# Attention and two MLP blocks on one core: a weight's split issued earlier, an addition moved to ScalarE, the sinks' split in two

## The chip, the cores and the metric

The kernel runs on one NeuronCore of a Trainium2 chip. Five engines work side by side, each through its own queue in order: TensorE (PE, matrix products and transposes into PSUM), VectorE (DVE), ScalarE (ACT), GpSimd (POOL) and SyncE (SP, which issues most of the DMAs). The metric is the device time of one execution in microseconds; lower is better.

## The reference

Attention with sink tokens and a sliding window (2 batches, 8 heads, 768 positions, head size 64), then two MLP blocks on the result:

```
scores = scale * q @ k^T, kept where pos < n_sink or 0 <= rel < window, else -1e9
a = exp(scores - max);  a = a / (sum(a) + 1e-9);  x = a @ v          # n_sink 4, window 128
h = relu(x @ w_in);  u, v = halves of h;  v = layernorm(v)           # 512 -> 1024
x = (u * (w_spatial @ v + b_spatial)) @ w_out
u = x + (relu(x^T @ w_tok1) @ w_tok2)^T;  out = u + relu(u @ w_ch1) @ w_ch2
```

The MLP weights arrive as 64-bit floats. The kernel decodes them to fp32 on the chip and then splits each into a high part (rounded to the PE's fp32r) and a low part (the rest), so that one product is three passes: high by high, high by low, low by high.

## The kernel before

**The attention loop.** `banded` (L339 on) walks over 12 blocks of 128 positions, two phases of four heads each, so over 24 steps g, in a software pipeline with one iteration n per step, n = -3 to 25. Iteration n does, in the order in which it is issued (and each engine takes its own part of that order):

- `sums(n+1)`: on DVE the row sums plus 1e-9 (L195) and their reciprocal (L196).
- `a_transpose(n)`, `a_out(n)`: PE transposes the probabilities `e` into the PSUM tile `tr`; ACT copies it to `aT` (L275), DVE writes a masked copy `aL` (L278; not in a batch's first block, so not in iterations 0, 1, 12 and 13).
- `norm(n+1)`: `e` times the reciprocal, two heads on POOL (L246), two on ACT (L250).
- `qk(n+3)`, `scores(n+3)`: PE products into the PSUM tiles `sc`; DVE masks, scales and takes the row minima (L213, L218).
- `expo(n+2)`: four exponentials on ACT with their row sums (L234; the sums are read out by an instruction of their own, ACTIVATION_READ_ACCUMULATOR).
- in even iterations `v_step` (POOL, `dv`, the difference of two blocks' values, L285) and `sink_parts` (ACT L257, POOL L258 and L259, tile `eS`).
- in iterations 1 and 13 `split_vs`: the sinks' values `vs`, of which ACT makes the high part (L156) and DVE the low part (L158), from the raw tile that a DMA brought. They are first read by `sinks_mm` in iterations 4 and 16.
- `step`: one further part of each layer norm under way (DVE L547; later ACT L550, POOL L551).
- in iterations -1 to 6 (`PUMPS`) `pump`: one 128x512 piece of `w_in` is decoded on DVE in three steps (L481, L485, L488) into `wi`; then `flush` splits the piece decoded one iteration **before**: high part by an ACT copy (L499), low part by a POOL subtraction (L500). The piece just decoded waits in `self.half`; the last one is flushed in iteration 7.
- `pv(n-1)`: products with the values into `pv`; in even iterations then `sinks_mm`, and `x_out`: ACT copies `pv` to the high part `xTH` (L329), DVE subtracts for the low part `xTL` (L330). The `pv` bank is single, so the next block's first product waits for `xTL`.
- in odd iterations `sinks`: PE transposes `eS` (tile `fl`), ACT copies it to `aS` (L313).
- `fill`: groups of three PE products of the first MLP layer (`psv`, `psu`), as many as a budget allows, once their rows of x are there. Their PSUM tiles share two banks with `fl`.

Iterations -1 to 6 therefore carry the decoding on DVE, iterations 3 on the fill products on PE. The order is that of the code; no scheduler changes it. A weight's raw tile is double (`bufs=2`), so the load of piece w+2 is issued on SP when piece w is decoded.

**The rest.** After the loop `mlp` runs the remaining layers. The change doesn't touch it.

Of the kernel before, what the change touches and what calls it, by code (L numbers as in the profile page):

```python
# [8 lines left out]
F32R = mybir.dt.float32r  # L9
I32 = mybir.dt.int32  # L10
U32 = mybir.dt.uint32
AF = mybir.ActivationFunctionType
ALU = mybir.AluOpType
PSUM = bass.MemoryType.PSUM

P = 128
B, H, S, D = 2, 8, 768, 64
NB = S // P
DM = H * D
# [5 lines left out]
SK = 8  # L25
SR = 3 * 4 * SK
# [3 lines left out]
NG = B * NB * 2  # L30

LQ, LE, LN = 3, 2, 1
PUMPS = range(-1, 7)
# [3 lines left out]
def f32(ap):  # L37
    return ap.bitcast(F32)


class Kernel:
# [106 lines left out]
            nc.sync.dma_start(out=raw[0:SR], in_=self.vs[b])  # L148
            self.vsraw = raw

    def split_vs(self, b):

        nc = self.nc
        raw = self.vsraw
        t = self.vsb[b] = self.ap.tile([P, DM], F32R, name="vs", tag="vs", bufs=1)
        nc.scalar.activation(out=t[0:SR], in_=raw[0:SR], func=AF.Copy)  # L156
        r = slice(4 * SK, 8 * SK)
        nc.vector.tensor_tensor(out=t[r], in0=raw[r], in1=f32(t[r]), op=ALU.subtract)  # L158

    def slots(self, j):  # L160

# [28 lines left out]
    def sums(self, g):  # L190

        V = self.nc.vector
        r = self.ap.tile([P, 4], F32, name="r", tag="r", bufs=3)
        self.rs[g] = r
        V.tensor_scalar(out=r, in0=self.sm[g], scalar1=1e-9, scalar2=None, op0=ALU.add)  # L195
        V.reciprocal(r, r)  # L196

    def scores(self, g):

# [23 lines left out]
    def expo(self, g):  # L223
        nc = self.nc
        j, ph = divmod(g, 2)
        i = j % NB
        u = KW if i else P
        s, nm = self.ss[g]
        if ph == 0:
            self.e[j] = self.ap.tile([P, H, KW], F32, name="e", tag="e", bufs=2)  # L230
        sm = self.ap.tile([P, 4], F32, name="sums", tag="sums", bufs=3)
        self.sm[g] = sm
        for c in range(4):
            nc.scalar.activation(  # L234
                out=self.e[j][:, 4 * ph + c, :u], in_=s[:, c, :u], func=AF.Exp, bias=nm[:, c : c + 1], scale=-1.0,
                accum_out=sm[:, c : c + 1],
            )

    def norm(self, g):

        nc = self.nc
        j, ph = divmod(g, 2)
        r = self.rs[g]
        w = KW if j % NB else P
        e = self.e[j][:, 4 * ph : 4 * ph + 4, 0:w]
        nc.gpsimd.tensor_tensor(  # L246
            out=e[:, 2:4], in0=e[:, 2:4], in1=r[:, 2:4].unsqueeze(2).to_broadcast([P, 2, w]), op=ALU.mult
        )
        for c in range(2):
            nc.scalar.activation(out=e[:, c], in_=e[:, c], func=AF.Copy, scale=r[:, c : c + 1])  # L250

    def sink_parts(self, j):

# [85 lines left out]
    def banded(self):  # L339
        self.q, self.vb, self.vsb, self.ps_s, self.ss, self.e, self.sm, self.rs = {}, {}, {}, {}, {}, {}, {}, {}  # L340
        self.aT, self.ps_x, self.aS, self.dv, self.eS = {}, {}, {}, {}, {}
        NJ = B * NB
        self.kr = self.ap.tile([P, NC4, RING, KW], F32, name="kr")
        self.vf = self.ap, "vf", 2
        self.scalar_loads(self.cp)
        self.load_qk(0, 2)
        self.warm(10)
        self.load_qk(1)
        self.prefetch()
        self.load_v(0)  # L350
        self.load_qk(2)
        self.masks(self.ap)
        for n in range(-LQ, NG + 2):
            j, ph = divmod(n, 2)
            self.xdone = self.xnext
            if ph and n >= -1:
                if (n + 7) // 2 < NJ:
                    self.load_qk((n + 7) // 2)
                if (n + 3) // 2 < NJ:
                    self.load_v((n + 3) // 2)  # L360
            if 0 <= n + LN < NG:
                self.sums(n + LN)
            if 0 <= n < NG:
                self.a_transpose(n)
                self.a_out(n)
            if 0 <= n + LN < NG:
                self.norm(n + LN)
            if n + LQ < NG:
                self.qk(n + LQ)
                if n < 0:  # L370
                    self.warm(3)
                self.scores(n + LQ)
            if 0 <= n + LE < NG:
                self.expo(n + LE)
            if 0 <= n < NG and ph == 0 and j % NB:
                self.v_step(j)
                self.sink_parts(j)
            if n in (1, 13):
                self.split_vs(n // 12)
            self.step()  # L380
            if n in PUMPS:
                self.pump()
            if n == max(PUMPS) + 1:
                self.flush()
            if 0 <= n - 1 < NG:
                self.pv(n - 1)
                if ph == 0:
                    if (j - 1) % NB:
                        self.sinks_mm(j - 1)

                    self.fill_until(j - 1)
                    self.x_out(j - 1)
            if 0 <= n < NG and ph == 1 and j % NB:
                self.sinks(j)
            if n == NG - 4:
                self.raws = [self.spatial_load(r) for r in range(2)]
            self.fill(BUDGET)
        self.xdone = self.xnext
        self.vf = self.sp, "tmp", 4
# [529 lines left out]
```

## Time and profile before

| | us |
|---|---|
| median of 3 runs | 494.08 (492.68 to 495.11) |
| the profiled execution | 494.1 |
| its span, first to last instruction | 492.3 |
| PE busy in the span | 469.2 (95%) |
| DVE, ACT, POOL busy | 281.2, 178.8, 146.7 |

The profile is of one execution; times of rows are us from the start of its span. The share of busy time over the whole span hides the stages: the attention loop takes about the first 145 us, the MLP the rest. In the table by stretches, PEclk is the granted TensorE clock as a share of 2.4 GHz, so 0.50 is 1.2 GHz.

### The profile page before, as it was taken

How to read it: one execution, taken by the hardware profiler on the slowest of the kernel's cores; microseconds unless marked ns; L12 is line 12 of the kernel's file. 1: busy time of each engine (PE TensorE's matmuls, PEld its weight loads, DVE VectorE, ACT ScalarE, POOL GpSimd, SP SyncE). 2: the span in 40 equal slices, each digit the busy share in tenths (PEclk: the TensorE clock that was granted, in tenths of full speed). 3: DMA queues.
4: the chain of work that ended last, by engine and by line, in shares of the span. 5: the costliest groups of instructions: out<-in, count | busy, mean ns of one | idle time of the engine just before them, and what ended most of it. 6: DMA issues, size and time to landing. Idle time of an engine off the chain costs nothing.

```text
span 492.3 us, 6952 instructions
## 1 busy us (share of the span) xinstructions
PE 469.2 (95%) x2562; PEld 392.3 (80%) x2562; DVE 281.2 (57%) x633; ACT 178.8 (36%) x483; POOL 146.7 (30%) x164
## 2 busy tenths in 40 slices
PE   8678899999999999999999989999999999999994
PEld 7356588788898999998888768888888888888883
DVE  5899865775555399937878698666412211311112
ACT  4656777787754323225642122222101210010000
POOL 1355752354354556642543033222100000000000
PEclk9859899999999999999999999999999999999998
DMA  8744132202005023303534044222010000200002
GB/s 258 246 151 152 66 101 95 87 22 87 1 30 185 1 85 87 102 6 116 173 119 137 35 129 128 91 94 73 21 66 1 0 1 0 86 1 0 1 0 92
DMA packets 19722, 38.48 MB, mean 78 GB/s; under 512 B 1824, under 2 KB 8224, under 8 KB 19680
## 3 DMA queue, kind: packets, MB, share of 16 engines
q1 hardware_dynamic: 19248, 37.69, 23.5%
q8 instruction: 22, 0.36, 0.3%
q10 hardware_dynamic: 432, 0.26, 0.2%
q14 instruction: 20, 0.16, 0.1%
HBM read 34.80 MB, written 3.15 MB: 77 GB/s over the span
## 4 chain that ended last, share of the span: by engine, by line
PE 81%; DVE 11%; ACT 5%; issue 1%; POOL 1%; POOLq 0%; ACTq 0%
PE pso L60 7%; PE pso L58 7%; PE pso L59 7%; PE psc L58 6%; PE psc L60 6%; PE psc L59 6%; PE psg L60 3%; PE psg L59 3%; PE psg L58 3%; PE pv L301 3%; PE ps L60 2%; PE ps L58 2%; PE ps L59 2%; ACT e L234 2%; DVE wi L485 2%; PE psu L58 2%
## 5 line engine op out<-in xcount | busy, mean ns | idle before, releaser
L647 DVE SCALAR_TENSOR_TENSOR hh<-psc,hh 128x512 fp32r<-128x512 f32 x36 | 24.9, 691 | 124.6 <-ACT hh L646 124.6
L646 ACT ACTIVATE hh<-psc 128x512 fp32r<-128x512 f32 x36 | 21.5, 597 | 156.0 <-PE psc L60 156.0
L60 PE MATMUL pso<-c2H,hh 128*128 128x512 f32 x144 | 56.3, 391 | 1.9 <-DVE hh L647 1.9
L58 PE MATMUL pso<-c2H,hh 128*128 128x512 f32 x144 | 56.8, 394 | 0.0
L59 PE MATMUL pso<-c2L,hh 128*128 128x512 f32 x144 | 56.1, 390 | 0.0
L488 DVE SCALAR_TENSOR_TENSOR wi<-rawi,wi 128x512 int32<-128x512 int32 (+2 forms) x46 | 40.3, 876 | 1.6
L234 ACT ACTIVATE e<-s,nm 128x136 f32<-128x136 f32 (+1 forms) x96 | 37.6, 393 | 3.9 <-DVE nm L218 3.9
L485 DVE SCALAR_TENSOR_TENSOR wi<-rawi,wi 128x512 int32<-128x512 int32 (+2 forms) x46 | 36.4, 791 | 1.6
L481 DVE TENSOR_SCALAR wi<-rawi 128x512 int32<-128x512 int32 (+2 forms) x46 | 33.4, 726 | 0.7 <-DMA rawi<-in_moe_w_ch 0.5
L60 PEld LDWEIGHTS pso<-c2H,hh 128*128 128x128 f32 x144 | 27.0, 188 | 8.0 <-DVE hh L647 2.3
L58 PE MATMUL psg<-wsTH,vnH 128*128 128x384 f32 x96 | 32.1, 334 | 0.0
L59 PE MATMUL psg<-wsTL,vnH 128*128 128x384 f32 x96 | 32.1, 334 | 0.0
L60 PE MATMUL psg<-wsTH,vnL 128*128 128x384 f32 x96 | 32.1, 334 | 0.0
L500 POOL TENSOR_TENSOR c2L<-wi,c2H 128x512 fp32r<-128x512 f32 x12 | 16.1, 1339 | 52.4 <-ACT c2H L499 52.4
L59 PEld LDWEIGHTS pso<-c2L,hh 128*128 128x128 f32 x144 | 27.1, 188 | 5.4
L58 PEld LDWEIGHTS pso<-c2H,hh 128*128 128x128 f32 x144 | 27.0, 188 | 5.3
L188 PE MATMUL sc<-kr,q 64*128 64x264 f32 (+2 forms) x192 | 28.8, 419 | 0.4 <-DVE nm L218 0.2
L60 PE MATMUL psc<-u2H,c 128*128 128x512 f32 x72 | 28.0, 389 | 0.0
L58 PE MATMUL psc<-u2H,c1H 128*128 128x512 f32 x72 | 28.0, 389 | 0.0
L59 PE MATMUL psc<-u2L,c1H 128*128 128x512 f32 x72 | 28.0, 389 | 0.0
L60 PE MATMUL psc<-u2H,c1L 128*128 128x512 f32 x72 | 28.0, 389 | 0.0
L58 PE MATMUL psc<-u2H,c 128*128 128x512 f32 x72 | 28.0, 389 | 0.0
(143 smaller groups left out, 1120.1 us busy)
## 6 DMA issues: line engine op xcount, KB each, us to landing
rawi<-in_moe_w_ch SPq DMA_DIRECT2D x24, 512.0 KB, 3.4
rawi<-in_moe_w_in SPq DMA_DIRECT2D x8, 512.0 KB, 4.5
v<-in_v SPq DMA_DIRECT2D x12, 256.0 KB, 3.6
out_x<-o SPq DMA_DIRECT2D x12, 256.0 KB, 2.4
kr<-in_k SPq DMA_DIRECT2D x11, 272.0 KB, 4.1
q<-in_q SPq DMA_DIRECT2D x11, 256.0 KB, 4.2
raws<-in_w_spT SPq DMA_DIRECT2D x6, 384.0 KB, 4.5
rawi<-in_moe_w_out SPq DMA_DIRECT2D x4, 512.0 KB, 5.2
```

What stands on the lines that cost most here:

```text
L58: self.nc.tensor.matmul(ps, lh, rh, start=(first and i == 0), stop=False)
L59: self.nc.tensor.matmul(ps, lh, rl, start=False, stop=False)
L60: self.nc.tensor.matmul(ps, ll, rh, start=False, stop=(last and i == n - 1))
L188: nc.tensor.matmul(o, q[r, p, :], k, start=True, stop=True)
L234: nc.scalar.activation(out=self.e[j][:, 4 * ph + c, :u], in_=s[:, c, :u], func=AF.Exp, bias=nm[:, c : c + 1], scale=-1.0, accum_out=sm[:, ...
L301: nc.tensor.matmul(ps[h * D : (h + 1) * D, p, :], w[:, (2 * p + h) * D : (2 * p + h + 1) * D], self.aT[g][c][:, 2 * x + h, :], start=(p == ...
L481: V.tensor_scalar(out=wi, in0=hi, scalar1=3, scalar2=0x3FFFFFFF, op0=ALU.logical_shift_left, op1=ALU.bitwise_and,)
L485: V.scalar_tensor_tensor(out=wi, in0=hi, scalar=-0x40000000, in1=wi, op0=ALU.bitwise_and, op1=ALU.bitwise_or)
L488: V.scalar_tensor_tensor(out=wi, in0=lo, scalar=29, in1=wi, op0=ALU.logical_shift_right, op1=ALU.bitwise_or)
L500: self.nc.gpsimd.tensor_tensor(out=dl, in0=w, in1=f32(dh), op=ALU.subtract)
L646: nc.scalar.activation(out=h, in_=ps, func=AF.Relu)
L647: nc.vector.scalar_tensor_tensor(out=l, in0=ps, scalar=0.0, in1=f32(h), op0=ALU.max, op1=ALU.subtract)
```

## The change

Three edits, all in the attention loop.

1. `flush` leaves `pump`'s place in the iteration. A piece decoded in iteration n is now split in iteration n+1 behind `a_out` and POOL's part of `norm`, and ahead of ACT's part of `norm`. For that `norm` gets an argument and is called twice.
2. 1e-9 is added to the row sums on ACT, right behind the exponentials that made them, instead of on DVE ahead of the reciprocal.
3. `split_vs` is done in two iterations: ACT's part in 2 and 14, DVE's in 3 and 15.

```diff
-    def split_vs(self, b):
+    def split_vs(self, b, part):
...
-        t = self.vsb[b] = self.ap.tile([P, DM], F32R, name="vs", tag="vs", bufs=1)
-        nc.scalar.activation(out=t[0:SR], in_=raw[0:SR], func=AF.Copy)
-        r = slice(4 * SK, 8 * SK)
-        nc.vector.tensor_tensor(out=t[r], in0=raw[r], in1=f32(t[r]), op=ALU.subtract)
+        if part == 0:
+            t = self.vsb[b] = self.ap.tile([P, DM], F32R, name="vs", tag="vs", bufs=1)
+            nc.scalar.activation(out=t[0:SR], in_=raw[0:SR], func=AF.Copy)
+        else:
+            t = self.vsb[b]
+            r = slice(4 * SK, 8 * SK)
+            nc.vector.tensor_tensor(out=t[r], in0=raw[r], in1=f32(t[r]), op=ALU.subtract)
...
-        V.tensor_scalar(out=r, in0=self.sm[g], scalar1=1e-9, scalar2=None, op0=ALU.add)
-        V.reciprocal(r, r)
+        V.reciprocal(r, self.sm[g])
...
+        nc.scalar.activation(out=sm, in_=sm, func=AF.Copy, bias=1e-9)
...
             if 0 <= n + LN < NG:
-                self.norm(n + LN)
+                self.norm(n + LN, "P")
+            if n - 1 in PUMPS:
+                self.flush()
+            if 0 <= n + LN < NG:
+                self.norm(n + LN, "A")
...
-            if n in (1, 13):
-                self.split_vs(n // 12)
+            if n in (2, 3, 14, 15):
+                self.split_vs(n // 12, n % 2)
             self.step()
             if n in PUMPS:
                 self.pump()
-            if n == max(PUMPS) + 1:
-                self.flush()
```

`norm(g, "P")` issues only POOL's instruction, `norm(g, "A")` only ACT's two. The orders of PE and SP stay as they were.

POOL in iterations 1 and 2 (`e` is the normalization, `wvL` a weight's low part, `dv` the difference of the values, `eS` the sinks' parts), before:

```order
L246 TENSOR_TENSOR e<-e,r 128x272
L500 TENSOR_TENSOR wvL<-wi,wvH 128x512
L246 TENSOR_TENSOR e<-e,r 128x272
L285 TENSOR_TENSOR dv<-v 128x512
L258 CAST eS<-eS 128x2x32
L259 TENSOR_TENSOR eS<-e,eS 128x2x32
L500 TENSOR_TENSOR wvL<-wi,wvH 128x512
```

and now:

```order
L250 TENSOR_TENSOR e<-e,r 128x272
L507 TENSOR_TENSOR wvL<-wi,wvH 128x512
L250 TENSOR_TENSOR e<-e,r 128x272
L507 TENSOR_TENSOR wvL<-wi,wvH 128x512
L290 TENSOR_TENSOR dv<-v 128x512
L263 CAST eS<-eS 128x2x32
L264 TENSOR_TENSOR eS<-e,eS 128x2x32
```

In the even iteration the subtraction has gone ahead of `dv` and `eS`; in the odd one it keeps its place in the row, and what it waits for (ACT's copy) comes earlier.

ACT in iterations 1 and 2 (`aT` is the transposes' eviction, `wvH` a weight's high part, `vs` the sinks' values), before:

```order
L275 ACTIVATE aT<-tr 128x512
L250 ACTIVATE e<-e,r 128x136 x2
L234 ACTIVATE e,sums<-s,nm 128x136 x4
L156 ACTIVATE vs<-vsraw 96x512
L499 ACTIVATE wvH<-wi 128x512
L275 ACTIVATE aT<-tr 128x512
L250 ACTIVATE e<-e,r 128x136 x2
L234 ACTIVATE e,sums<-s,nm 128x136 x4
L257 ACTIVATE eS<-e 128x2x32
L499 ACTIVATE wvH<-wi 128x512
L329 ACTIVATE xTH<-pv 128x4x128
```

and now:

```order
L280 ACTIVATE aT<-tr 128x512
L506 ACTIVATE wvH<-wi 128x512
L255 ACTIVATE e<-e,r 128x136 x2
L236 ACTIVATE e,sums<-s,nm 128x136 x4
L240 ACTIVATE sums<-sums 128x4
L280 ACTIVATE aT<-tr 128x512
L506 ACTIVATE wvH<-wi 128x512
L255 ACTIVATE e<-e,r 128x136 x2
L236 ACTIVATE e,sums<-s,nm 128x136 x4
L240 ACTIVATE sums<-sums 128x4
L262 ACTIVATE eS<-e 128x2x32
L157 ACTIVATE vs<-vsraw 96x512
```

The copy of the weight moved from the iteration's end to between `aT` and the normalization, each four exponentials have an addition behind them, and `vs` went one iteration on.

DVE between the scores of iteration 1 and the masked copy `aL` of iteration 2, before:

```order
L218 ISA nm 128x1
L158 TENSOR_TENSOR vs<-vsraw,vs 32x512
L481 TENSOR_SCALAR wi<-rawi 128x512
L485 SCALAR_TENSOR_TENSOR wi<-rawi,wi 128x512
L488 SCALAR_TENSOR_TENSOR wi<-rawi,wi 128x512
L195 TENSOR_SCALAR r<-sums 128x4
L196 RECIPROCAL r<-r 128x4
L278 TENSOR_TENSOR aL<-tr,lowT 128x512
```

and now:

```order
L220 ISA nm 128x1
L488 TENSOR_SCALAR wi<-rawi 128x512
L492 SCALAR_TENSOR_TENSOR wi<-rawi,wi 128x512
L495 SCALAR_TENSOR_TENSOR wi<-rawi,wi 128x512
L198 RECIPROCAL r<-sums 128x4
L283 TENSOR_TENSOR aL<-tr,lowT 128x512
```

The subtraction of the sinks' values went to iteration 3, ahead of its decoding, and the addition is gone from every iteration.

## Rows read from the trace of the kernel before

**Rows 1.** Busy time by stretches: us, engines (instructions), granted clock, DMA share, GB/s
```profile
21.40:35.00 13.60, 9.36 (x48) 6.35 (x47) 12.21 (x36) 8.92 (x32) 6.74 (x8) 0.50 0.43 144
35.00:55.20 20.20, 16.38 (x129) 11.63 (x128) 19.42 (x56) 13.21 (x45) 12.58 (x15) 1.00 0.40 132
55.20:58.60 3.40, 3.40 (x21) 2.87 (x22) 3.30 (x11) 1.53 (x7) 3.10 (x5) 0.52 0.01 2
58.60:110.00 51.40, 50.56 (x399) 40.52 (x399) 33.59 (x144) 39.30 (x141) 23.05 (x35) 1.00 0.23 73
110.00:492.30 382.30, 373.69 (x1871) 318.78 (x1869) 196.83 (x314) 105.08 (x223) 96.44 (x90) 1.00 0.19 63
```

**Rows 2.** Waits of PE, whole span: waited for, us in total, times, longest
```profile
PE pv L301 <- DVE xTL L330: 4.4, 4, 1.6
...
PE tr L267 <- DVE aL L278: 3.5, 2, 3.3
```

**Rows 3.** DVE by line, 14.0 to 55.2 us: busy us, mean ns, idle before
```profile
L488 DVE SCALAR_TENSOR_TENSOR wi<-rawi,wi 128x512 int32<-128x512 int32 x8 | 7.5, 935 | 0.3
...
L485 DVE SCALAR_TENSOR_TENSOR wi<-rawi,wi 128x512 int32<-128x512 int32 x7 | 5.8, 832 | 0.2
...
L481 DVE TENSOR_SCALAR wi<-rawi 128x512 int32<-128x512 int32 x7 | 4.0, 577 | 0.0
...
L195 DVE TENSOR_SCALAR r<-sums 128x4 f32<-128x4 f32 x7 | 2.6, 378 | 0.0
```

**Rows 4.** DVE in order of time: start, duration, instruction, idle time and its releaser
```profile
22.39 0.68 DVE L158 TENSOR_TENSOR vs<-vsraw,vs 32x512 fp32r<-32x512 f32 x1 [1.13 <-ACT vs L156]
...
30.36 0.68 DVE L330 TENSOR_TENSOR xTL<-pv,xTH 128x512 fp32r<-128x512 f32 x1
...
35.30 1.68 DVE L488 SCALAR_TENSOR_TENSOR wi<-rawi,wi 128x512 int32<-128x512 int32 x1
...
37.46 0.69 DVE L278 TENSOR_TENSOR aL<-tr,lowT 128x512 f32<-128x512 f32 x1 [0.19 <-ACT aT L275]
...
49.98 0.16 DVE L195 TENSOR_SCALAR r<-sums 128x4 f32<-128x4 f32 x1
50.18 0.18 DVE L196 RECIPROCAL r<-r 128x4 f32<-128x4 f32 x1
...
52.65 0.42 DVE L481 TENSOR_SCALAR wi<-rawi 128x512 int32<-128x512 int32 x1
53.11 0.69 DVE L485 SCALAR_TENSOR_TENSOR wi<-rawi,wi 128x512 int32<-128x512 int32 x1
53.84 0.69 DVE L488 SCALAR_TENSOR_TENSOR wi<-rawi,wi 128x512 int32<-128x512 int32 x1
54.45 0.68 DVE L330 TENSOR_TENSOR xTL<-pv,xTH 128x512 fp32r<-128x512 f32 x1
...
90.90 0.68 DVE L158 TENSOR_TENSOR vs<-vsraw,vs 32x512 fp32r<-32x512 f32 x1 [0.75 <-ACT vs L156]
```

**Rows 5.** POOL in order of time
```profile
34.78 1.65 POOL L500 TENSOR_TENSOR wvL<-wi,wvH 128x512 fp32r<-128x512 f32 x1 [2.18 <-ACT wvH L499]
...
51.03 1.27 POOL L285 TENSOR_TENSOR dv<-v 128x512 f32<-128x512 f32 x1
```

**Rows 6.** ACT in order of time
```profile
28.45 0.19 ACT L234 ACTIVATION_READ_ACCUMULATOR e<-s,nm 128x1 f32 x1
28.55 0.24 ACT L257 ACTIVATE eS<-e 128x64 fp32r<-128x64 f32 x1
```

**Rows 7.** Waits of ACT, 14.0 to 55.2 us
```profile
ACT e L250 <- DVE r L196: 13.2, 6, 3.0
```

**Rows 8.** PE in order of time
```profile
69.29 0.44 PE L58 MATMUL psu<-xTH,wuH 128*128 128x384 f32 x1 [0.57 <-ACT aS L313]
...
107.93 0.44 PE L301 MATMUL pv<-aT,v 128*64 128x128 f32 x4 [0.18 <-DVE xTL L330]
```

**Rows 9.** DMA issues by line: count, KB each, median us to landing
```profile
rawi<-in_moe_w_in SPq DMA_DIRECT2D x8, 512.0 KB, 4.5
```

More of the change, by code (lines that the diff above doesn't have):

```diff
@@ L237, in expo, with norm @@
             )
-    def norm(self, g):
+        nc.scalar.activation(out=sm, in_=sm, func=AF.Copy, bias=1e-9)
+    def norm(self, g, on):
         nc = self.nc
@@ L245, in norm @@
         e = self.e[j][:, 4 * ph : 4 * ph + 4, 0:w]
[L246 to L250, printed above, removed]
+        if on == "P":
+            nc.gpsimd.tensor_tensor(
+                out=e[:, 2:4], in0=e[:, 2:4], in1=r[:, 2:4].unsqueeze(2).to_broadcast([P, 2, w]), op=ALU.mult
+            )
+        else:
+            for c in range(2):
+                nc.scalar.activation(out=e[:, c], in_=e[:, c], func=AF.Copy, scale=r[:, c : c + 1])
     def sink_parts(self, j):
```

## The prediction

> **What bounds the kernel now.** I read the table by stretches first, since the shares of the whole span hide the stage in question. From 35.0 to 55.2 us VectorE (DVE) is busy 19.42 of 20.20 us and TensorE (PE) 16.38; from 21.4 to 35.0 it is DVE 12.21 of 13.60 and PE 9.36, at a granted clock of 0.50 (1.2 of 2.4 GHz). From 58.6 us to the end PE is busy 50.56 of 51.40 and 373.69 of 382.30 us [rows 1]. So there are two stages: in iterations 0 to 6 of the attention loop DVE sets the pace, and from iteration 7 on PE does. PE's order isn't touched by the change, and after the hand-over its work is a fixed sum. The time therefore moves by as much as the hand-over moves, plus any new wait of PE behind it. PE's waits say where the hand-over is: 4.4 us of waits for xTL (up to 1.6 at once) and 3.5 for aL, both made by DVE [rows 2]; the last large one ends when the xTL of iteration 6, started at 54.45 us, is done [rows 4].
>
> Then I asked what DVE does in those 40 us that it need not do. Grouped by line, the 7 additions of 1e-9 (L195) take 378 ns in the mean where an undisturbed one takes 160; the decoding steps L481, L485 and L488 take 577, 832 and 935 ns where iteration 6 shows 420, 690 and 690 [rows 3, 4]. One pair shows why: L488 starts at 35.30 and lasts 1.68 us, to 36.98, while GpSimd (POOL) runs its weight subtraction from 34.78 for 1.65 us, to 36.43 [rows 4, 5]. If L488 needs its 0.69 it began at 36.29, 0.14 us before POOL's end: it stood still for POOL. DVE's work on PSUM doesn't: POOL's dv subtraction at 51.03 lies beside the scores, which fill their 2.47 us from the reciprocal at 50.18 to L481 at 52.65 [rows 4, 5].
>
> **The change part by part**, summed on DVE's path from iteration 0 to the xTL at 54.45.
>
> *Collisions taken away.* L195: 7 x (0.378 - 0.16) = 1.5. L481: 7 x (0.577 - 0.42) = 1.1. L485: 7 x (0.832 - 0.69) = 1.0. L488: 8 x (0.935 - 0.69) = 2.0. Sum 5.6 us [rows 3, 4]. The subtraction that made them now follows POOL's share of the normalization, 0.85 us behind the reciprocal (50.18 to 51.03), and lies beside the scores.
>
> *The addition leaves DVE.* From L195 to the reciprocal is 0.20 us (49.98 to 50.18) [rows 4]; 7 of them give 1.4.
>
> *The sinks' values.* DVE waits 1.13 us for ScalarE's (ACT) copy at 22.39 [rows 4]. With the copy an iteration earlier the wait goes; the subtraction (0.68, so 0.7 from start to start) stays, in iteration 3. Together with the two parts above: 8.1 us off DVE's path.
>
> *Collisions put in.* In iterations 2, 4 and 6 POOL now does normalization, weight subtraction and dv before anything else. Counted from the reciprocal: subtraction from 0.85, 1.27 long (the time of the equally shaped dv [rows 5]), so to 2.12; dv to 3.39. DVE wants L481 at 2.47 and gets it at 3.39 - 0.14 = 3.25: 0.78 each, 2.3 for three. In iterations 0 and 1 there is no aL, so that L481 comes about 0.6 earlier (aL's 0.69 less the overlap), at 1.9, against the subtraction's release at 2.12 - 0.14 = 1.98: 0.2 for both. In iteration 5 a layer norm's two small POOL operations come first; I put 0.4. Sum 2.9.
>
> *PE becomes late next.* Before, aL at 37.46 starts 7.10 us behind the xTL at 30.36, and waits 0.19 there [rows 4]. In between PE runs from xTL over the product with v and three fill groups to the transposes that aL reads, mostly at half clock (0.50 from 21.4 to 35.0 [rows 1]). DVE's way there falls to 0.6 (xTL, 0.68 less the overlap) + 2.47 + 0.7 (sinks) + 1.80 (decoding, 52.65 to 54.45) + 0.10 = 5.7. With PE's side as slow as it was, DVE waits 1.4 where it waited 0.19: 1.2 lost.
>
> Hand-over: 8.1 - 2.9 - 1.2 = 4.0 us earlier.
>
> *What ACT pays.* Its 24 additions of 1e-9 are an operation that the trace doesn't show. Lower bound: the 64-column ACTIVATE at 28.55 lasts 0.24, and successive ones overlap by about 0.10, so 0.14. The addition reads what the accumulator read at 28.45 leaves, and that ends 0.09 after ACT could have started [rows 6]; with 0.05 allowed for the signal that is 0.28. Upper bound: the 0.24 unoverlapped, plus 0.09, twice over for a full stop of the pipe, 0.66. I take 0.28, since both of its parts are read from neighbours. While DVE bounds, ACT's idle time covers it: it waits for the reciprocal 13.2 us in six waits there [rows 7]. Later it shows at three places: PE waits 0.57 for aS at 69.29, and I count the same place two iterations on as just covered so far; 0.28 each, 0.6. And at 107.93 PE waits 0.18 for an xTL [rows 8] at the end of an ACT-DVE chain through iterations 13 to 16: four additions (+1.1), three L195 less (-0.6), the sinks' copy moved from 13 to 14, where the subtraction at 90.90 (0.68, waited 0.75 [rows 4]) leaves the chain (about -0.2): +0.3. Together 0.9.
>
> *Copies earlier on ACT.* The weight's copy (a 128x512 ACTIVATE) now stands before the normalization. ACT mostly waits for the reciprocal there, so it can hold the normalization up by no more than its own length, and DVE's 2.47 us of scores cover that. If the transposes come late, copy and subtraction come late with them (rival 2). Loads: decoding ends earlier, and each weight's load is issued at that point; 4.5 us to land [rows 9], against an iteration of about 5 us plus 2.47 of scores. Covered; nothing.
>
> Sum: 4.0 - 0.9 = 3.1 us. The profiled execution took 494.1 us (span 492.3, 1.8 around it), the median of the three is 494.08, so both give the same: **491.0 us**.
>
> A page speaks against one part: the Trainium skill's "ScalarE: Activation LUTs", section "Rules for kernel authors", puts additions on VectorE, not ScalarE. Its section "What ACT_TABLE_LOAD costs" gives 186 ns and 0.833 ns a column for an ACTIVATE with an immediate bias; for 64 columns that is 0.24 us, as the trace has it; for 4 it is an estimate of 0.19 us, by which the sum wouldn't move. The rule holds here only if ACT is what is late (rival 3), and the trace shows what the addition costs on DVE beside POOL.
>
> **Rivals.** 1: *the half clock eats the gain.* PE's first half-rate stretch, 21.4 to 35.0, follows its idle time there, the second (55.2 to 58.6, 0.52) follows the waits for xTL [rows 1, 2]. If the first ends no earlier on the clock on the wall although the work comes 3 to 4 us sooner, then the last 1.5 us of PE's way from xTL to the transposes, which ran at full rate behind 35.0, doubles: 492.5. For it: DVE's waits stay, so PE still idles. Against it: it idles less.
>
> 2: *the subtraction is late again.* Copy and subtraction stand behind aT, and aT behind PE's transposes; where PE is late (iterations 4 to 6) they slide into the decoding, and dv behind them. One more 0.78 in two of these iterations: 492.6. It would also be that the change doesn't do what it says.
>
> 3, the other side: *ACT becomes the chain.* With x for one addition on ACT the sum is 4.0 - 2x - (4x - 0.8) = 4.8 - 6x. At 0.28 it is the forecast, at 0.8 nothing is left, at 1.2 it is -2.4: 496.5. This mechanism alone makes the kernel slower, from 0.8 us an addition on, over the upper bound. The page's rule named above would end here.
>
> 4: *the clock holds.* If PE idles so little that it isn't slowed, the 1.2 of aL and some 1.6 of the second stretch (3.4 us at 0.52) go too: 488.2.
>
> **How the numbers follow.** Forecast 0.50, rival 1 0.17, rival 2 0.13, rival 3 0.08, rival 4 0.12. Around the forecast I allow 1.3 either way for the sizes of the new collisions. About 0.5% (2.5 us) is what a measurement tells from no change, so faster means below 491.6: two thirds of the forecast, rival 4 and a fifth of rivals 1 and 2, 0.33 + 0.12 + 0.06 = 0.51; slower, rival 3 and a remainder, 0.09; the rest, 0.40, within. The range goes from rival 4 to the far end of rivals 1 and 2, 488.2 to 494.2; it leaves out rival 3 and what lies beyond the ends, under 2 in 10.
>
> **What would show it.** Decoding steps of undisturbed length except L481 in iterations 2, 4 and 6, there about 0.8 longer; POOL's weight subtraction beside the scores; no wait at the sinks' subtraction; a wait of DVE for aT near iteration 4; the addition on ACT with under 0.3 us to the next start; the xTL of iteration 6 at 50 to 51 us instead of 54.45; PE's waits for aS a little longer. I am wrong if the collisions merely change their victim in every iteration, if PE's half-rate stretches grow, or if ACT's idle time for reciprocals vanishes.

## The result, and the profile after

| | before | after |
|---|---|---|
| median of the runs | 494.08 us | 489.55 us (5 runs, 488.62 to 490.71) |
| ratio | | 0.9908, 95% interval 0.9885 to 0.9931 |
| profiled execution | 494.1 us, span 492.3 | 488.62 us, span 486.8 |
| mean granted clock of PE | 0.979 | 0.989 |
| xTL of iteration 6 starts | 54.45 us | 48.34 us |

The change gains 4.5 us where 3.1 were forecast. The profiled execution is the fastest of its five, so that the two profiles lie 5.5 us apart.

Line numbers moved: the reciprocal is now L198 (there is no addition on DVE), decoding L488, L492 and L495, `aL` L283, xTL L335, the sinks' subtraction L161, POOL's weight subtraction L507, `dv` L290, ACT's addition L240.

The table by stretches of the changed kernel (us; busy time and instructions of PE, PEld, DVE, ACT, POOL; granted clock, DMA share, GB/s) answers to [rows 1]:

```profile
15.60:18.30 2.70, 2.70 (x14) 1.54 (x14) 2.60 (x10) 2.42 (x10) 0.80 (x2) 0.50 0.96 277
18.30:49.30 31.00, 23.27 (x192) 16.67 (x190) 30.12 (x93) 25.60 (x90) 20.20 (x24) 1.00 0.56 182
49.30:52.70 3.40, 3.40 (x22) 2.77 (x19) 3.30 (x15) 2.74 (x12) 2.90 (x5) 0.50 0.01 2
52.70:58.60 5.90, 5.90 (x46) 4.72 (x45) 2.75 (x13) 3.93 (x16) 2.60 (x5) 1.00 0.25 75
```

DVE still sets the pace up to the hand-over (30.12 of 31.00 us busy). The stretch at half rate that lay over 21.4 to 35.0 us is now 2.7 us long and ends at 18.3; the one behind the hand-over is as long as before, 3.4 us.

DVE by line from 14.0 to 48.4 us, with the three decoding steps of iterations 0 to 6 (busy us, mean ns, idle before), then POOL in iteration 2 and DVE in iterations 2 to 4 and 6, in order of time. They answer to [rows 3 to 5]:

```profile
L488 DVE TENSOR_SCALAR wi<-rawi 128x512 int32<-128x512 int32 x7 | 5.5, 782 | 0.0
L492 DVE SCALAR_TENSOR_TENSOR wi<-rawi,wi 128x512 int32<-128x512 int32 x7 | 4.8, 692 | 0.2
L495 DVE SCALAR_TENSOR_TENSOR wi<-rawi,wi 128x512 int32<-128x512 int32 x7 | 4.8, 692 | 0.2
...
L198 DVE RECIPROCAL r<-sums 128x4 f32<-128x4 f32 x6 | 1.0, 165 | 0.0
```

```profile
22.09 1.29 POOL L507 TENSOR_TENSOR wvL<-wi,wvH 128x512 fp32r<-128x512 f32 x1
23.34 1.27 POOL L290 TENSOR_TENSOR dv<-v 128x512 f32<-128x512 f32 x1
```

```profile
23.71 1.18 DVE L488 TENSOR_SCALAR wi<-rawi 128x512 int32<-128x512 int32 x1
...
29.44 0.68 DVE L161 TENSOR_TENSOR vs<-vsraw,vs 32x512 fp32r<-32x512 f32 x1
...
32.04 0.66 DVE L283 TENSOR_TENSOR aL<-tr,lowT 128x512 f32<-128x512 f32 x1
...
45.76 1.20 DVE L488 TENSOR_SCALAR wi<-rawi 128x512 int32<-128x512 int32 x1
...
48.34 0.68 DVE L335 TENSOR_TENSOR xTL<-pv,xTH 128x512 fp32r<-128x512 f32 x1
```

Two of the three decoding steps take their undisturbed 0.69. L488 takes 1.18 to 1.20 in iterations 2, 4 and 6: in iteration 2 it starts at 23.71, needs 0.42 and ends at 24.89, so it ran from 24.47, 0.14 us before `dv` ends on POOL (23.34 + 1.27 = 24.61). The sinks' subtraction (L161) and the `aL` of iteration 4 wait for nothing.

ACT in order of time in iteration 2, and the waits of ACT from 14.0 to 50.8 us ([rows 6, 7]); then PE's waits over the whole span ([rows 2]), and three places of PE behind the hand-over ([rows 8]):

```profile
23.97 0.19 ACT L236 ACTIVATION_READ_ACCUMULATOR e<-s,nm 128x1 f32 x1
24.19 0.20 ACT L240 ACTIVATE sums<-sums 128x4 f32<-128x4 f32 x1
24.30 0.24 ACT L262 ACTIVATE eS<-e 128x64 fp32r<-128x64 f32 x1
```

```profile
ACT wvH L506 <- DVE wi L495: 2.2, 4, 1.3
ACT wuH L506 <- DVE wi L495: 1.9, 3, 1.1
ACT e L255 <- DVE r L198: 1.7, 2, 0.8
```

```profile
PE pv L306 <- DVE xTL L335: 7.0, 4, 2.4
...
PE psu L58 <- ACT aS L318: 1.1, 2, 0.8
```

```profile
63.43 0.44 PE L58 MATMUL psu<-xTH,wuH 128*128 128x384 f32 x1 [0.80 <-ACT aS L318]
...
73.84 0.44 PE L58 MATMUL psu<-xTH,wuH 128*128 128x384 f32 x1 [0.32 <-ACT aS L318]
...
102.65 0.44 PE L306 MATMUL pv<-aT,v 128*64 128x128 f32 x4 [0.53 <-DVE xTL L335]
```

Without the addition ACT could have gone on at 24.06, as the accumulator read at 23.97 lets its successor start after 0.09; it went on at 24.30. One addition costs 0.24. It is paid where ACT is late: 0.57 of waiting for aS became 0.80 + 0.32, and 0.18 for an xTL became 0.53.

### The profile page after: what moved, and what is told of

Same layout as the page of the kernel before. It is cut to its first block, busy times and chain, and to the rows that moved or that the text cites. A ratio compares the mean times of both kernels' runs of the same rounds, so it can differ in the third digit from the quotient of the medians.

```text
span 486.8 us, 6920 instructions
## 1 busy us (share of the span) xinstructions
PE 465.2 (96%) x2562; PEld 389.8 (80%) x2562; DVE 275.2 (57%) x609; ACT 183.5 (38%) x507; POOL 145.0 (30%) x164
## 4 chain that ended last, share of the span: by engine, by line
PE 80%; DVE 12%; ACT 4%; issue 1%; DMA 1%; POOL 1%; POOLq 0%; ACTq 0%
PE pso L60 7%; PE pso L58 7%; PE pso L59 7%; PE psc L60 6%; PE psc L58 6%; PE psc L59 6%; PE psg L59 3%; PE psg L60 3%; PE psg L58 3%; PE pv L306 3%; PE ps L59 2%; PE ps L58 2%; PE ps L60 2%; PE psu L58 2%; DVE wi L492 2%; PE sc L191 2%
## 5 line engine op out<-in xcount | busy, mean ns | idle before, releaser
L495 DVE SCALAR_TENSOR_TENSOR wi<-rawi,wi 128x512 int32<-128x512 int32 (+2 forms) x46 | 39.2, 853 | 1.6
L492 DVE SCALAR_TENSOR_TENSOR wi<-rawi,wi 128x512 int32<-128x512 int32 (+2 forms) x46 | 36.4, 791 | 1.6
L488 DVE TENSOR_SCALAR wi<-rawi 128x512 int32<-128x512 int32 (+2 forms) x46 | 33.6, 730 | 1.3 <-DMA rawi<-in_moe_w_ch 0.7
L58 PE MATMUL psg<-wsTH,vnH 128*128 128x384 f32 x96 | 32.1, 334 | 0.0
L59 PE MATMUL psg<-wsTL,vnH 128*128 128x384 f32 x96 | 32.1, 334 | 0.0
L60 PE MATMUL psg<-wsTH,vnL 128*128 128x384 f32 x96 | 32.1, 334 | 0.0
L507 POOL TENSOR_TENSOR c2L<-wi,c2H 128x512 fp32r<-128x512 f32 x12 | 15.8, 1313 | 52.8 <-ACT c2H L506 52.8
L191 PE MATMUL sc<-kr,q 64*128 64x264 f32 (+2 forms) x192 | 27.6, 405 | 0.6 <-DVE nm L220 0.5
```

The costliest lines, as they stand in the source:

```text
L58: self.nc.tensor.matmul(ps, lh, rh, start=(first and i == 0), stop=False)
L59: self.nc.tensor.matmul(ps, lh, rl, start=False, stop=False)
L60: self.nc.tensor.matmul(ps, ll, rh, start=False, stop=(last and i == n - 1))
L191: nc.tensor.matmul(o, q[r, p, :], k, start=True, stop=True)
L488: V.tensor_scalar(out=wi, in0=hi, scalar1=3, scalar2=0x3FFFFFFF, op0=ALU.logical_shift_left, op1=ALU.bitwise_and,)
L492: V.scalar_tensor_tensor(out=wi, in0=hi, scalar=-0x40000000, in1=wi, op0=ALU.bitwise_and, op1=ALU.bitwise_or)
```

## Experiments

My theory: what moves the time is DVE's path to the xTL of iteration 6, and on it the standing still for POOL. Rival A: the instructions taken off DVE are the gain, and POOL always finds a victim. Rival B: PE's clock is.

### The three parts one by one and in pairs

Six kernels hold one or two of the parts; with before and after they are all eight combinations. The flush alone (`e1_flush_only`) and the addition alone (`e2_add_only`), each against before:

```
...
-                self.norm(n + LN)
+                self.norm(n + LN, "P")
+            if n - 1 in PUMPS:
+                self.flush()
+            if 0 <= n + LN < NG:
+                self.norm(n + LN, "A")
...
-            if n == max(PUMPS) + 1:
-                self.flush()
```

```
-        V.tensor_scalar(out=r, in0=self.sm[g], scalar1=1e-9, scalar2=None, op0=ALU.add)
-        V.reciprocal(r, r)
+        V.reciprocal(r, self.sm[g])
...
+        nc.scalar.activation(out=sm, in_=sm, func=AF.Copy, bias=1e-9)
```

> The kernel before with one part of the change alone: a weight's high and low part are issued behind POOL's share of the next iteration's normalization; the addition stays on DVE, the sinks' copy and subtraction stay in one iteration. Theory (DVE standing still for POOL's subtraction is the largest item): 5.6 us of standing still go, 2.9 come in, so the xTL of iteration 6 starts 2.7 us earlier, at 51.7 instead of 54.45, the additions on DVE take 0.16 each, and the time is 494.1 - 2.7 = 491.4 us. Rival A (the gain is the instructions taken off DVE, and what POOL does only changes its victim): xTL at 54.4, 494.1 us. Rival B (the gain is PE's clock): the time follows the length of the half-rate stretches, whatever xTL does.

> The kernel before with one part alone: 1e-9 is added on ScalarE. Theory: the seven additions cost DVE 7 x 0.20 and stood still for POOL another 1.5 us; the reciprocal that now stands first doesn't stand still, so xTL of iteration 6 starts 2.9 earlier, at 51.5; ACT's additions cost 0.9 later; 494.1 - 2.0 = 492.1 us. The decoding steps stay as long as in the kernel before (577, 832, 935 ns). Rival A: only the 1.4 us of the instructions go, xTL at 53.0, the reciprocal takes over the standing still; 494.1 - 1.4 + 0.9 = 493.6 us. Rival B: follows the half-rate stretches.

The split alone (`e3_split_only`) is this edit, with the two halves of the function as in the change; `e4_add_split` has the second and the third edit:

```
...
-            if n in (1, 13):
-                self.split_vs(n // 12)
+            if n in (2, 3, 14, 15):
+                self.split_vs(n // 12, n % 2)
```

> The kernel before with one part alone: the sinks' copy one iteration earlier than the subtraction. Theory and rival A alike: the wait of 1.13 us goes, xTL of iteration 6 at 53.3, 494.1 - 1.1 = 493.0 us. If the copy finds ACT busy and only moves the wait, xTL stays at 54.4 and the time at 494.1.

> The changed kernel with the weight's parts issued where they were before (addition on ScalarE and split sinks stay). Theory: 2.9 + 1.1 = 4.0 off DVE, xTL of iteration 6 at 50.4, ACT pays 0.9, 494.1 - 3.1 = 491.0 us, and the flush's 2.7 are missing from the changed kernel's gain or come twice (if both together are worth less than one by one). Rival A: the whole gain is here, 489.6 us, xTL at 48.4. Rival B: follows the half-rate stretches.

Later came the remaining two pairs: `e11_flush_split` has the first and third edit, `e12_flush_add` the first and second.

> The changed kernel with the addition back on DVE. By the parts as the single runs showed them: DVE has 7 x 0.20 = 1.4 more, none of it standing still for POOL (the flush's early place sees to that); ACT has 24 additions less, which by run e7_add4's slope (7.2 us for 0.72 more each) may be worth up to 2.4 us, mostly behind the hand-over. Theory: xTL of iteration 6 at 49.7 and 490.0 us, that is the addition's move is worth 0.5 us once the flush has moved. Rival A (the addition's move is the change's whole gain): 492.0 us, as after the split alone.

> The changed kernel without the split of the sinks' values (copy and subtraction in one iteration, as before): the last of the eight combinations of the three parts. Theory (the split takes a wait off DVE's path that nothing else takes off): DVE waits 1.3 us for the sinks' copy, as in the runs with the flush or the addition alone; xTL of iteration 6 at 49.6, 489.5 + 1.3 = 490.8 us; should PE's half-rate stretch then fall on iteration 3, a wait for aT of 1.0 to 1.6 us as in those runs, 492 us. Rival (any two of the three do what all three do, as the pairs addition with split and flush with split did): 489.5 us.

| kernel | ratio to before (95%) | path | standing still | wait for the sinks' copy | wait for aT, it. 4 | additions | rest |
|---|---|---|---|---|---|---|---|
| before | 1 | 40.10 | 5.55 | 1.13 | 0.19 | 1.2 | 32.0 |
| flush | 0.9974 (0.9960 to 0.9987) | 38.19 | 2.39 | 1.30 | 1.26 | 1.2 | 32.0 |
| addition | 0.9952 (0.9934 to 0.9970) | 38.16 | 3.08 | 1.31 | 1.64 | 0 | 32.1 |
| split | 0.9966 (0.9950 to 0.9982) | 37.77 | 4.62 | 0 | 0 | 1.2 | 32.0 |
| addition + split | 0.9907 (0.9886 to 0.9928) | 34.58 | 2.50 | 0 | 0 | 0 | 32.1 |
| flush + split | 0.9919 (0.9895 to 0.9943) | 36.88 | 2.58 | 0 | 1.03 | 1.2 | 32.1 |
| flush + addition | 0.9964 (0.9949 to 0.9980) | 38.80 | 2.48 | 1.74 | 2.61 | 0 | 32.0 |
| all three (after) | 0.9908 (0.9885 to 0.9931) | 34.64 | 2.75 | 0 | 0 | 0 | 31.9 |

All columns but the ratio are us from the profiled executions. "Path" runs from DVE's reciprocal in iteration 0 to the start of the xTL of iteration 6. "Standing still" is what DVE's additions, decoding steps and layer norm scaling in it last beyond 0.16, 0.42, 0.69 and 0.54 us each; "additions" are six at 0.20. The rest is path less the four columns. It is 31.9 to 32.1 throughout: the columns account for DVE's path, in all eight kernels.

Set beside what was expected: the flush alone gained half of its 2.7 us (0.0026 of 494 is 1.3), and a wait for aT of 1.26 us came in; the addition alone gained 2.4 where 2.0 was expected, the split alone 1.7 where 1.1 was; addition + split had its xTL at 48.28, which is rival A's 48.4 and not the theory's 50.4; flush + split took its time as expected (0.9919 of 494.08 is 490.1), with the xTL at 50.78 instead of 49.7; flush + addition came out at the theory's worse case, with the wait for aT.

Three things follow. First, the flush move isn't the only thing that takes standing still away: alone it brings 5.55 down to 2.39, but with addition and split and without it, it falls to 2.50 as well, and the time is that of the full change. The trace of addition + split, POOL and DVE in order of time, shows how:

```profile
25.24 1.72 POOL L503 TENSOR_TENSOR wvL<-wi,wvH 128x512 fp32r<-128x512 f32 x1
...
29.66 1.56 POOL L503 TENSOR_TENSOR wvL<-wi,wvH 128x512 fp32r<-128x512 f32 x1 [2.09 <-ACT wvH L502]
...
36.89 1.29 POOL L503 TENSOR_TENSOR wuL<-wi,wuH 128x512 fp32r<-128x512 f32 x1
```

```profile
26.35 0.16 DVE L198 RECIPROCAL r<-sums 128x4 f32<-128x4 f32 x1
...
30.09 1.66 DVE L488 SCALAR_TENSOR_TENSOR wi<-rawi,wi 128x512 int32<-128x512 int32 x1
...
36.66 0.68 DVE L333 TENSOR_TENSOR xTL<-pv,xTH 128x512 fp32r<-128x512 f32 x1
```

In the odd iteration 3 the subtraction, issued at its old place, meets the decoding (1.66 instead of 0.69). In the even iteration 4 it starts at 36.89, beside xTL, the reciprocal and `aL`, and nobody lengthens. In the kernel before an addition stood beside a subtraction and was held up (L195, 378 ns in the mean, [rows 3]), most of all in iteration 1:

```profile
18.02 1.23 DVE L195 TENSOR_SCALAR r<-sums 128x4 f32<-128x4 f32 x1
```

The reciprocal isn't held up. So flush move and addition both take the additions' standing still away (1.55 of the 5.55); each without the other leaves 2.4 to 3.1 us, both together 2.5 to 2.75. What is left is of another kind in either case: without the move it is POOL's subtraction against the decoding of odd iterations (0.97 and 1.10 us in iterations 3 and 5 of addition + split), with it POOL's `dv` against L488 of even ones (1.18 to 1.20 instead of 0.42, above). Rival A is right in that the move brings nothing measurable on top of addition and split (0.9908 against 0.9907), and wrong in that the standing still is no constant: it halves.

Second, the split is the one part without a substitute: no kernel without it comes below 0.995, and with either other part beside it the whole gain is there, as far as the intervals tell. It takes away more than its wait. PE and DVE in order of time in flush + addition, with two stretches of that kernel, and PE's transposes at the same place in the changed kernel:

```profile
25.20 1.20 PE L269 MATMUL tr<-ident,e 128*128 128x128 f32 x4 [3.69 <-DVE sc L212]
```

```profile
21.59 0.68 DVE L158 TENSOR_TENSOR vs<-vsraw,vs 32x512 fp32r<-32x512 f32 x1 [1.74 <-ACT vs L156]
...
36.83 0.69 DVE L280 TENSOR_TENSOR aL<-tr,lowT 128x512 f32<-128x512 f32 x1 [2.61 <-ACT aT L277]
```

```profile
25.30:34.80 9.50, 8.04 (x36) 5.77 (x37) 8.68 (x29) 6.53 (x26) 5.81 (x7) 0.50 0.59 193
34.80:46.00 11.20, 10.04 (x81) 7.61 (x80) 8.93 (x30) 8.47 (x30) 6.52 (x9) 1.00 0.50 165
```

```profile
22.34 0.85 PE L272 MATMUL tr<-ident,e 128*128 128x128 f32 x4 [1.19 <-DVE sc L215]
```

DVE's 1.74 us for the copy and 0.68 for the subtraction stand between iteration 2's transposes and iteration 3's on PE. PE idles 3.69 us there, and 1.19 in the changed kernel. Behind that idle time the granted clock is 0.50 (1.2 GHz) up to 34.8, and DVE waits 2.61 us for the aT of iteration 4. That the idle time brought the clock down isn't tested in this pair.

Third, rival B is a term and not the whole: after has no wait for aT at all and addition + split neither; flush + split has 1.03 and still most of the gain. The runs tell clock and path apart: at the same mean granted clock of 0.982 to 0.983 the kernel before took 492.1 to 493.8 us (30 runs), flush + split 489.6 to 490.7 (4 runs) and flush + addition 491.6 to 493.7 (11 runs). And in the profiled runs flush + split has more time at half rate than flush + addition (13.6 against 10.2 us, worked out from the granted clock of 14 to 62 us) and is the faster one.

### What is left of the standing still

`e6_no_dv` leaves out POOL's `dv` in iterations 2, 4 and 6, so that part of the product is another; `e5_mixed_flush` gives each iteration its own place for the flush; `e9_mixed_early` does so in iteration 0 too. Against after:

```
+        if j in (1, 2, 3):
+            self.dv[j] = self.vb[j]
+            return
```

```
-            if n - 1 in PUMPS:
+            if n - 1 in PUMPS and ph:
```

```
-            if n - 1 in PUMPS:
+            if n - 1 in PUMPS and (ph or n < 2):
```

> The changed kernel, with POOL's dv subtraction left out in iterations 2, 4 and 6 (v itself stands in dv's place there, so part of the attention's product is another); it measures what is left of the standing still. Theory: L488 takes 0.42 instead of 1.20 in each of the three iterations, 2.3 us in all; xTL of iteration 6 at 46.0, 487.2 us. Rival A: the sinks' parts that follow on POOL take dv's place beside the decoding, L488 or L492 stay long, 489.5 us. Rival C: DVE then waits for aT about 1 us, 488.2 us.

> The changed kernel, with a weight's parts issued behind the normalization in odd iterations alone; in even ones, where POOL also has dv and the sinks' parts, they stay behind the decoding as in the kernel before. Theory (what counts is whether POOL's subtraction meets DVE's work on PSUM or DVE's decoding, iteration by iteration): of the changed kernel's 2.75 us of standing still 0.78 goes in each of the iterations 2, 4 and 6, and at most 0.4 comes in, as the subtraction there falls beside xTL and the reciprocal; xTL of iteration 6 at 46.3 instead of 48.34, 489.5 - 2.0 = 487.5 us. Rival A (the subtraction always finds a victim): xTL at 48.3, 489.5 us. Rival C (DVE gets free and waits for aT instead): POOL no longer holds DVE, but a wait of DVE for aT of about 1 us appears; 488.5 us.

> The kernel of run e5_mixed_flush with the early place also in iteration 0, which has no dv either. There DVE's L488 of iteration 1 stood still for 1.05 us because the late subtraction of iteration 0 pushed the next one down to 19.21. Theory: 1.05 goes and 0.2 comes in (the changed kernel's own L488 of 0.51 and 0.54 in iterations 0 and 1), xTL of iteration 6 at 46.4 instead of 47.26, 487.7 - 0.8 = 486.9 us. Rival (PE's half-rate stretch falls differently and DVE waits for aT in iteration 4): up to 1.3 us of wait, 488.0 us.

The kernel before took 492.5 to 494.1 us in the median beside these kernels, so the ratios are what is compared.

| kernel | median | ratio to before (95%) | path | standing still | wait for aT | rest |
|---|---|---|---|---|---|---|
| after | 489.55 | 0.9908 (0.9885 to 0.9931) | 34.64 | 2.75 | 0 | 31.9 |
| e5_mixed_flush | 487.73 | 0.9883 (0.9859 to 0.9906) | 33.50 | 1.28 | 0 | 32.2 |
| e6_no_dv | 487.10 | 0.9862 (0.9828 to 0.9896) | 33.63 | 0.44 | 1.04 | 32.2 |
| e9_mixed_early | 486.09 | 0.9868 (0.9838 to 0.9897) | 32.67 | 0.45 | 0 | 32.2 |

Without `dv`, L488 takes 0.42 in iterations 2, 4 and 6, so it was `dv` that held it; the wait for aT of rival C comes in, 1.04 us. DVE in order of time in `e9_mixed_early`, iterations 2, 4 and 6:

```profile
23.71 0.42 DVE L488 TENSOR_SCALAR wi<-rawi 128x512 int32<-128x512 int32 x1
...
33.81 0.42 DVE L488 TENSOR_SCALAR wi<-rawi 128x512 int32<-128x512 int32 x1
...
44.40 0.42 DVE L488 TENSOR_SCALAR wi<-rawi 128x512 int32<-128x512 int32 x1
...
46.36 0.69 DVE L335 TENSOR_TENSOR xTL<-pv,xTH 128x512 fp32r<-128x512 f32 x1
```

All three are back at 0.42 with all of POOL's work still done: the early place is good where POOL has nothing else, the late one where `dv` and the sinks' parts come first. The xTL came at 46.36 where 46.4 was expected, and at 47.26 in `e5_mixed_flush` where 46.3 was: there I had overlooked iteration 0, whose late subtraction pushed the next one into iteration 1's decoding (1.47 instead of 0.42). `e9_mixed_early` is the fastest kernel that does all the work, 1.3% below before. Against after it gains 2.0 us by the ratios (0.0040 of 494); their intervals overlap, so what shows the gain is the path, 1.97 us shorter. Its six times are 485.1 to 489.2 us; the longest came with a mean granted clock of 0.982, the others with 0.985 to 0.993. That PE's clock made the 3 us between is likely, but not shown.

### Is the wait for aT the clock's doing?

`e10_no_dv_warm` is `e6_no_dv` with ten matmuls more:

```
                 if n < 0:
                     self.warm(3)
+                if n == 3:
+                    self.warm(10)
```

> The kernel of run e6_no_dv (dv left out in iterations 2, 4 and 6) with 10 matmuls on the identity issued on PE in iteration 3, where it waited 1.66 us for xTL and the granted clock then fell to 0.50 from 27 to 30 us. It asks whether the new wait of DVE for aT in iteration 4 (1.04 us) is the half-rate clock's doing. Theory: the clock stays at 1.00 there, PE's way from xTL to the transposes shrinks from 4.9 to 3.4 us as in the changed kernel, the wait for aT goes, xTL of iteration 6 at 46.8 instead of 47.88, 487.1 - 1.0 = 486.1 us. Rival (PE's own work is what is late): the clock holds and the wait stays at 1.0, or grows as the matmuls are in the way; 487.1 us or more.

DVE and stretches of `e6_no_dv`, then of `e10_no_dv_warm` (the latter of PE alone: us, busy, clock, DMA share, GB/s):

```profile
33.02 0.69 DVE L283 TENSOR_TENSOR aL<-tr,lowT 128x512 f32<-128x512 f32 x1 [1.04 <-ACT aT L280]
```

```profile
26.70:30.00 3.30, 3.14 (x20) 2.69 (x21) 3.18 (x14) 3.11 (x13) 1.88 (x2) 0.51 0.73 257
```

```profile
31.69 0.69 DVE L283 TENSOR_TENSOR aL<-tr,lowT 128x512 f32<-128x512 f32 x1 [0.21 <-ACT aT L280]
```

```profile
24.00:27.00 3.00, 3.00 (x24) 1.00 0.92 294
27.00:30.00 3.00, 3.00 (x28) 1.00 0.56 175
```

PE is busy through the time in which it had waited for xTL, the clock stays at 1.00 (2.4 GHz), the wait falls from 1.04 to 0.21 and the path from 33.63 to 32.83. So 0.83 of the wait was the clock's. On the whole time this isn't resolved: ratio 0.9852 (0.9821 to 0.9882) against 0.9862 (0.9828 to 0.9896).

### What an addition on ACT costs

`e7_add4` against after:

```
         nc.scalar.activation(out=sm, in_=sm, func=AF.Copy, bias=1e-9)
+        for _ in range(3):
+            nc.scalar.activation(out=sm, in_=sm, func=AF.Copy, bias=0.0)
```

> The changed kernel with three further additions (of 0) on ScalarE behind each one of 1e-9, 0.24 each. It prices the addition and asks how much ACT has in hand. By the prediction's sum, 4.8 - 6x, x grows by 0.72 and the time by 4.3 us, to 493.9: two waits of PE for aS grow by 0.72 each, the chain of iterations 13 to 16 by 4 x 0.72; xTL of iteration 6 stays at 48.3. Rival (ACT has nothing in hand while DVE bounds, since each reciprocal waits for ACT's last sum): xTL of iteration 6 goes back by 0.72 in each of 8 iterations, 5.8 us, to 54.1, and the time by 6 us or more, to 495.5 or more. Rival (ACT has in hand everywhere but at aS): 491.0 us.

Measured: 496.76 us, ratio 1.0060 (1.0037 to 1.0083), 7.5 us over after by the ratios (0.0152 of 494). PE in order of time, the same three places as above:

```profile
65.08 0.45 PE L58 MATMUL psu<-xTH,wuH 128*128 128x384 f32 x1 [2.29 <-ACT aS L320]
...
76.59 0.45 PE L58 MATMUL psu<-xTH,wuH 128*128 128x384 f32 x1 [1.39 <-ACT aS L320]
...
107.87 0.70 PE L308 MATMUL pv<-aT,v 128*64 128x128 f32 x4 [1.94 <-DVE xTL L337]
```

The path grew by 1.7 us (36.30; DVE waits 1.07 for aT in iteration 4, with the clock at 0.50 from 30 to 32), the waits for aS by 1.49 and 1.07, the one for xTL by 1.41, and one of 0.50 for xTL came at 95.10: 6.1 of the 7.5. My slope of 6x is too small: it gave 4.3 us, and the rival with the path not free (495.5 or more) is nearer. Up to two groups of additions stand ahead of an aS (1.49 is 2.07 times 0.72), where I had counted one, and the path isn't free. The slope is 7.5 / 0.72 = 10.4 us per us, and by an estimate from this one point nothing would be left of the change's 4.5 us from 0.24 + 4.5 / 10.4 = 0.67 us an addition on, not 0.8.

### xTL ahead of the decoding

`e8_x_first` against after moves `self.pump()` in iterations 2, 4 and 6:

```
-            if n in PUMPS:
+            if n in PUMPS and (ph or n < 2):
                 self.pump()
...
                     self.x_out(j - 1)
+                    if n in PUMPS and n >= 2:
+                        self.pump()
```

> The changed kernel with the decoding of iterations 2, 4 and 6 issued behind xTL instead of ahead of it. Theory (PE is bound from the hand-over on, and the hand-over is the xTL of iteration 6): that xTL starts 1.8 us earlier, at about 46.5, PE's 7.0 us of waits for xTL fall to about 2, and the time falls by what of it isn't waited for again at the next aL: between 0 and 1.8, I take 1.0: 488.5 us. Rival (DVE's sum of work up to the aL of iteration 7 is the hand-over, not xTL): PE's waits move from xTL to aL, and the time stays at 489.5.

Measured: 491.22 us, ratio 0.9948 (0.9928 to 0.9967), slower than after by 2.0 us in the ratios, which neither side expected. The intervals just overlap (after reaches 0.9931); that it loses shows in the xTL of iteration 6, at 49.52 where 46.5 was expected and after has 48.34. DVE in order of time:

```profile
49.52 0.69 DVE L335 TENSOR_TENSOR xTL<-pv,xTH 128x512 fp32r<-128x512 f32 x1 [1.79 <-ACT xTH L334]
```

xTL subtracts ACT's xTH, and ACT reaches that only behind its exponentials, so DVE stood idle (4.8 us in the three iterations) for time that the decoding had filled. I had taken PE's long wait for xTL as a sign that xTL could start earlier, without asking what xTL itself needs.

## Why the prediction was right, point by point

*What bounds.* Right. In all kernels but `e7_add4` and `e8_x_first`, the profiled time less the start of that xTL is 438.8 to 440.6 us, while the xTL moves over 8.1 us (46.36 to 54.45): the time follows the hand-over.

*Collisions taken away, 5.6, and put in, 2.9.* As sizes right: 5.55 measured in the kernel before, 2.75 after, at the places and lengths named (0.76, 0.78, 0.78 in iterations 2, 4, 6; 0.09 and 0.12 in iterations 0 and 1; 0.22 in iteration 5, at the layer norm's scaling instead of L488). As a cause wrong: the prediction has the subtraction's new place take the 5.6 away, and the pairs show that without it 2.50 are left as well. That the sum held all the same is luck of a kind: the change contained both remedies, so it made no difference which of them was given the credit.

A rule that fits the standing still is on a page of the Trainium skill, "SBUF — State Buffer", section "Who interferes with whom": VectorE and GpSimd share a port pair; an instruction of VectorE that needs it (a mode with both ports, or two inputs in SBUF against a GpSimd instruction that reads SBUF) and one of GpSimd exclude each other for the whole instruction. The trace agrees as far as it shows, with DVE going on 0.14 us before the recorded end on POOL; it doesn't show the port.

*The addition leaves DVE, 1.4; the sinks' wait, 1.13.* Right in the trace (six additions, 1.2 us, lie on the path as the table counts it, the seventh just ahead of its start); the single runs show that the addition's going also spares its standing still and that the split spares PE's idle time.

*PE becomes late next, 1.2.* This is the step that failed. No wait for aT came in the changed kernel, and the 0.19 went. The step took PE's way from xTL to the transposes to be as slow as before, with its first stretch at half rate over it; that stretch ended at 18.3 us. PE needs 3.4 us from the product with v to the transposes where `e6_no_dv`, at half rate, needs 4.9 and the kernel before 5.1 (31.10 to 36.20). PE in order of time, after and then `e6_no_dv`:

```profile
27.01 0.44 PE L306 MATMUL pv<-aT,v 128*64 128x128 f32 x4 [2.35 <-DVE xTL L335]
...
30.38 0.60 PE L272 MATMUL tr<-ident,e 128*128 128x128 f32 x4
```

```profile
26.86 0.69 PE L309 MATMUL pv<-aT,v 128*64 128x128 f32 x4 [1.66 <-DVE xTL L338]
...
31.75 0.60 PE L272 MATMUL tr<-ident,e 128*128 128x128 f32 x4
```

The mechanism exists: six of the runs have the wait, 1.0 to 2.6 us, each with a granted clock of 0.50 in some stretch between 26 and 34 us; the split alone has that clock too and no wait, probably because its DVE is later by 4.62 us of standing still.

*Hand-over, 4.0.* It was 6.1, and the xTL came at 48.34 where 50 to 51 was named: the 1.2 that didn't come and the 0.19 that went make 1.4, the start-up was 0.45 us faster (which needn't be the change's doing: with the same code up to there the reciprocal of iteration 0 comes at 13.70 after and at 14.25 in `e6_no_dv`), and 0.3 are the collisions' 2.75 and roundings.

*What ACT pays, 0.9.* Right in sum and place: aS 0.57 to 0.80 + 0.32, xTL 0.18 to 0.53, together 0.90 of the 6.1; the profiled execution is 5.5 shorter, so some 0.3 came back where I didn't follow it. The addition occupies 0.24, not 0.28; by the prediction's own 6x that is worth 0.2 us, so a shorter addition does move the sum a little, which the prediction denied. Its slope was wrong, as `e7_add4` showed.

A rule of the Trainium skill spoke against this part: "ScalarE: Activation LUTs", section "Rules for kernel authors", keeps additions on VectorE. With flush and split in place both ways take about the same time (0.9919 against 0.9908, each interval nearly 0.005 wide); these runs don't tell the two ways apart, for the rule or against it, although the hand-over of the profiled runs is 2.4 us earlier with the addition on ACT (48.34 against 50.78).

*The rivals.* 1 and 2 didn't happen: there is no half rate from 18.3 to 49.3, and no further collision came. 3 is real and steeper than I had it. 4 happened for the first stretch and not for the second. Of what I named as a sign of being wrong, one came and meant nothing: ACT's waits for the reciprocal fell from 13.2 [rows 7] to 1.7, because ACT now waits for the decoding with its weight copies (4.1) at an earlier point, and is busier.

*The sum.* 491.0 forecast, 489.55 measured; of the 1.4 between, the term on PE is worth as much in the profiled run. Since the changed kernel's runs spread over 2.1 us, I can't say that every run has it so.

## What to carry to other kernels

Price a stall once per cause and not once per remedy: two of the three parts took the additions' standing still away, and only leaving each out in turn showed which was needed. When two engines block each other, give the blocking instruction the place that suits each iteration's own load, rather than one place for all; here that took 1.97 us more off DVE's path, and 2.0 us off the time by ratios whose intervals overlap. A wait in a stage that another engine bounds needn't be free if PE idles through it: look at the granted clock of the next iterations (in `e10_no_dv_warm` filling one such wait kept it at 1.00).

## What the runs showed of the hardware

- DVE's instructions stood still for POOL by kind. The 128x4 addition from SBUF was held for up to 1.1 us and the 128x512 decoding steps for up to 1.1; the reciprocal of 128x4 never (0.14 to 0.18 in all fourteen traces; in addition + split it took 0.16 at 26.35, amid POOL's subtraction from 25.24 to 26.96), nor the work that reads PSUM (`aL` 0.65 to 0.69 throughout).
- Where the granted clock falls isn't read from one idle time. After, PE idled 2.35 us ahead of 27.01 and the clock stayed at 1.00; in `e6_no_dv` it idled 1.66 us at the same place and the clock went to 0.50. What each had done earlier differs; I can't name the rule from these runs.
